# Reordering the operations of a head pair in a threshold attention kernel: turning back and normalization first, v product among the transposes

## The chip, the cores and the metric

The kernel runs on one core of one Trainium2 chip. The metric is the device time of one execution in microseconds, median of three runs; lower is better. TensorE (PE in the rows) multiplies matrices and transposes, VectorE (DVE), ScalarE (ACT) and GpSimd (POOL) work element by element, SyncE (SP) issues most DMA transfers. Each engine works through its own queue in program order.

## The reference

Two stages follow each other. The first is an attention whose weights below a threshold are set to zero, the second sends each token through one of eight small networks, chosen by a hash of its id.

```python
# q, k, v: (8, 8, 576, 64) f32; tau = 0.02
scores = matmul(q, k.T) / sqrt(64)
scores = where(scores >= max(scores) - tau, scores, -1e9)
attn = exp(scores - max(scores))
attn = attn / (sum(attn) + 1e-9)
x = (attn @ v) as (batch * seq, heads * head_dim)   # 4608 x 512
for e in range(8):                                   # expert = hash(token id) % 8
    out[mask_e] = relu(x[mask_e] @ w1[e]) @ w2[e]    # 512 -> 1024 -> 512
```

## The kernel before

The attention half takes two heads of one batch at a time: a head pair p, 32 of them. The 576 rows of q are cut into five steps s: step 0 holds the last 64 rows of both heads, stacked to 128 partitions (one "head" of work), steps 1 to 4 hold 128 rows of each head (two heads of work). The steps of all pairs form one sequence n = 5p + s, and the loop over n is a software pipeline that is written out by hand: each engine gets its instructions in the order in which the loop body names them. One pass of the loop body does work of several ages:

- `score(n + 1)` on TensorE: 288 columns at a time into the PSUM tile sc, of which there are two (line 168).
- `negate(n)` on VectorE: reads sc, writes the negated scores ns and their minimum nmx (line 180); GpSimd makes the threshold thr from it (line 184).
- `expo(n, j)` on ScalarE: w = exp of ns (line 191).
- `mask(n - 1, j)` on VectorE: sets weights beyond thr to zero and sums the rest into rs (line 204).
- `turn_w(n - 2, j)` on TensorE: ten transposes of 64 columns into the one PSUM tile tr (line 215); `put_wT` on ScalarE copies tr to wT_a (steps 0 to 2) or wT_b (steps 3 and 4) (line 233).
- `av_part(p - 1, g, chunks)` on TensorE: the product with v for the pair before, in two groups g (0 with wT_a, 1 with wT_b) over five chunks of keys, into the PSUM tile av, one bank for each group (line 241). `put_oT` on ScalarE copies a finished group to oT (line 247).
- `turn_o` on TensorE, in step 0: transposes oT of the pair p - 2 back into the same tile av (line 215). `put_x(p - 2)`, at the end of step 0, adds 1e-9 to the sums (line 256), takes the reciprocal rec (line 258), multiplies on VectorE to xm (line 261) and on ScalarE, twice, to xt (line 268), and stores xm and xt on SP to x_scratch in DRAM (lines 270, 273).

There is one tile av, and it is used in turn for the product of a pair and for what is turned back. SP also loads q, k and v of later pairs, in step 0, and GpSimd scales q of the next pair in step 1 (line 148). From n = 7 on, each pass ends with one piece of the routing computation (`route`), mostly on VectorE; four of its pieces also put two multiplications of 128 x 648 elements on GpSimd (line 396), and four put nine matmuls into tr. The pieces end in pair 6. After the loop, the experts' half gathers rows of x_scratch and is a long series of matmuls (lines 537 and 551).

Of the kernel before, what the change touches and what calls it, by code (L numbers as in the profile page):

```python
# [9 lines left out]
FP32 = mybir.dt.float32  # L10
# [4 lines left out]
ALU = mybir.AluOpType  # L15
# [5 lines left out]
def kernel(  # L21
# [12 lines left out]
    nc = tc.nc  # L34

    B, H, D, S = qT.shape
    N, DIN = out.shape
    E, _, F = w1.shape
    P = 128
    HP = H // 2  # L40
    NP = B * HP
# [7 lines left out]
    TAIL = NQ * P  # L49
# [15 lines left out]
    x_dram = nc.dram_tensor("x_scratch", (N, DIN), FP32, kind="Internal").ap()  # L65
# [32 lines left out]
    with tc.tile_pool(name="a_q", bufs=1) as a_q, \  # L98
# [21 lines left out]

        oT = a_o.tile([P, 64 + S], FP32, name="oT")
        av = ps_av.tile([P, 2, 512], FP32, name="av")
        kts, rss, scs, nss, stats, ws = {}, {}, {}, {}, {}, {}

        def load_pair(p):
            b, hp = divmod(p, HP)
# [24 lines left out]
        def heads(n):  # L151
            return 1 if n % NS == 0 else 2

        def score(n):


            p, s = divmod(n, NS)
            q_sb, k_sb = q_bufs[p % 3], kts[p]
            for j in range(heads(n)):
                sc = ps_sc.tile([P, 2, 512], FP32, name="sc")  # L160
                scs[n, j] = sc
            for i in range(2):
                for j in range(heads(n)):
                    if s == 0:
                        rows, cols = slice(0, P), slice(TAIL, TAIL + P)
                    else:
                        rows, cols = slice(64 * j, 64 * j + 64), slice(P * (s - 1), P * s)
                    nc.tensor.matmul(scs[n, j][:, i, 0:S2], lhsT=q_sb[rows, cols],  # L168
                                     rhs=k_sb[rows, S2 * i:S2 * i + S2], start=True, stop=True)

        def negate(n):

            nmx = a_st.tile([P, 2], FP32, name="nmx")
            thr = a_st.tile([P, 2], FP32, name="thr")
            stats[n] = (nmx, thr)
            for j in range(heads(n)):
                sc = scs.pop((n, j))
                ns = a_ns.tile([P, S], FP32, name="ns")
                nss[n, j] = ns
                nc.vector.tensor_scalar(out=ns[:].rearrange("p (i s) -> p i s", i=2),  # L180
                                        in0=sc[:, :, 0:S2], scalar1=-1.0, scalar2=None,
                                        op0=ALU.mult, op1=ALU.min, accum_out=nmx[:, j:j + 1])
            nj = heads(n)
            nc.gpsimd.tensor_scalar(out=thr[:, 0:nj], in0=nmx[:, 0:nj], scalar1=drop[:],  # L184
                                    scalar2=None, op0=ALU.add)

        def expo(n, j):
            w = w_bufs[w_count[0] % NW]
            w_count[0] += 1
            ws[n, j] = w  # L190
            nc.scalar.activation(w[:, 0:S], nss[n, j][:], AF.Exp, bias=stats[n][0][:, j:j + 1],  # L191
                                 scale=-1.0)
# [27 lines left out]
        def turn_w(n, j):  # L220
            tr = ps_tr.tile([P, 2, 512], FP32, name="tr")
            turn(tr, ws.pop((n, j)), KCOLS)
            return tr

        def put_wT(n, j, tr):
            s = n % NS
            src = tr[:, :, 0:64 * NC].rearrange("p r (c q) -> p r c q", c=NC)
            if s == 0:
                dst = wT[0][:, :, :, 0:64]
            else:  # L230
                c0 = 64 + P * (s - 1) if s < 3 else P * (s - 3)
                dst = wT[s // 3][:, j, :, c0:c0 + P].rearrange("p c (r q) -> p r c q", r=2)
            nc.scalar.copy(dst, src)  # L233

        def av_part(p, g, chunks):


            width = (WA, WB)[g]
            for c in chunks:
                for j in range(2):  # L240
                    nc.tensor.matmul(av[64 * j:64 * j + 64, g, 0:width],  # L241
                                     lhsT=v_bufs[p % 3][:, c, 64 * j:64 * j + 64],
                                     rhs=wT[g][:, j, c, :], start=(c == 0), stop=(c == NC - 1))

        def put_oT(g):
            c0, width = ((64, WA), (64 + WA, WB))[g]
            nc.scalar.copy(oT[:, c0:c0 + width], av[:, g, 0:width])  # L247
# [1 line left out]
        def turn_o():  # L249
            turn(av, oT, [(P * (t + 1), P * (t + 1)) for t in range(NQ)] + [(64, 0)])  # L250

        def put_x(p):

            b, hp = divmod(p, HP)
            rec = a_st.tile([P, 9], FP32, name="rec")
            nc.vector.tensor_scalar(out=rec[:], in0=rss.pop(p)[:], scalar1=1e-9, scalar2=None,
                                    op0=ALU.add)
            nc.vector.reciprocal(rec[:], rec[:])
            xm = a_x.tile([P, NQ, P], FP32, name="xm")
            xt = a_x.tile([P, D], FP32, name="xt")  # L260
            nc.vector.tensor_tensor(
                out=xm[:].rearrange("p t (j d) -> p t j d", j=2),
                in0=av[:, :, 0:4 * D].rearrange("p j (t d) -> p t j d", t=NQ),
                in1=rec[:, 0:8].rearrange("p (t j) -> p t j", j=2)[:, :, :, None]
                .to_broadcast([P, NQ, 2, D]), op=ALU.mult)
            for j in range(2):
                half = slice(64 * j, 64 * j + 64)
                nc.scalar.mul(xt[half, :], av[half, j, 4 * D:5 * D], rec[half, 8:9])  # L268
            r0, c0 = b * S, hp * P
            nc.sync.dma_start(  # L270
                out=x_dram[r0:r0 + TAIL, c0:c0 + P].rearrange("(t p) m -> p t m", p=P), in_=xm[:])
            for j in range(2):
                nc.sync.dma_start(out=x_dram[r0 + TAIL:r0 + S, c0 + D * j:c0 + D * j + D],
                                  in_=xt[64 * j:64 * j + 64, :])

        def route():

# [106 lines left out]
            for c0 in range(0, NTC, M):  # L384
# [25 lines left out]
                else:  # L410
# [10 lines left out]
                          in_=bass.AP(tensor=tau.tensor, offset=0, ap=[[0, P], [1, 1]]))  # L421
        for q_sb in q_bufs:
# [6 lines left out]
                          in_=bass.AP(tensor=dataclasses.replace(token_ids.tensor,  # L429
                                                                 shape=[2 * N], dtype=I32),  # L430
                                      offset=0, ap=[[2 * NTC, P], [2, NTC], [1, 2]]))
# [4 lines left out]
                                op0=ALU.is_ge)  # L436
        nc.vector.tensor_scalar(out=drop[:], in0=keep_any[:], scalar1=-3e38, scalar2=3e38,
                                op0=ALU.mult, op1=ALU.add)
# [17 lines left out]
        LAST = NS * NP  # L456
        pieces = route()
        with tc.manual_schedule():
            for xg in xg_bufs:
                nc.gpsimd.memset(xg[:], 0.0)  # L460
            score(0)
            for n in range(LAST + NS + 1):
                p, s = divmod(n, NS)
                m = n - 2
                if s == 0 and p + 2 < NP:
                    load_pair(p + 2)
                if s == 0 and p + 1 < NP:
                    load_v(p + 1)
                if s == 1 and p + 1 < NP:
                    scale_q(p + 1)  # L470
                if s == 2 and p in (20, 24):
                    load_w1(p // 4 - 5)
                if s == 2 and p in (22, 26):
                    load_w2((p - 22) // 4)

                done = p - 1
                av_ok = 0 <= done < NP
                if av_ok and s in (1, 2):
                    av_part(done, 0, ((0, 1), (2, 3, 4))[s - 1])
                if av_ok and s in (3, 4):  # L480
                    av_part(done, 1, ((0, 1, 2), (3, 4))[s - 3])
                back = p - 2 if s == 0 else -1
                if back >= 0:
                    turn_o()

                turned = 0 <= m < LAST
                if turned:
                    tr = turn_w(m, 0)
                if n < LAST:
                    negate(n)  # L490
                    expo(n, 0)
                if turned:
                    put_wT(m, 0, tr)
                if n < LAST and heads(n) == 2:
                    expo(n, 1)
                if n + 1 < LAST:
                    score(n + 1)
                if 0 < n <= LAST:
                    for j in range(heads(n - 1)):
                        mask(n - 1, j)  # L500
                if av_ok and s in (2, 4):
                    put_oT(s // 2 - 1)
                if turned and heads(m) == 2:
                    tr = turn_w(m, 1)
                    put_wT(m, 1, tr)
                if back >= 0:
                    put_x(back)
                if n >= NS + 2:
                    next(pieces, None)

    with tc.tile_pool(name="m_x", bufs=2) as m_x, \
# [78 lines left out]
        with tc.For_i(0, n_ov, 1) as it:  # L590
# [5 lines left out]
                out=w1_sb[:],  # L596
                in_=w1[bass.ds(ex, 1)].rearrange("o (c p) f -> p (o c) f", p=P))
# [45 lines left out]
```

## Time and profile before

| | |
|---|---|
| time, median of 3 runs | 1199.1 us (1198.03 to 1199.86) |
| profiled execution: time, span | 1200.82 us, 1199.2 us |
| PE busy | 1082.9 us, 90% |
| DVE busy | 527.9 us, 44% |
| ACT busy | 482.4 us, 40% |
| POOL busy | 256.1 us, 21% |
| mean granted TensorE clock | 0.98 |

The profile shows one execution. The shares are over the whole span; the attention half ends around 605 us, the rest is the experts' half, in which TensorE is busy nearly all the time. So the shares of the attention half have to be read from its own stretch, and the order of waits from single pairs. A busy time of TensorE includes the modelled end of the last matmul of a series, so the distance between the starts of two groups says more than the busy time of one.

### The profile page before, as it was taken

How to read it: one execution, taken by the hardware profiler on the slowest of the kernel's cores; microseconds unless marked ns; L12 is line 12 of the kernel's file. 1: busy time of each engine (PE TensorE's matmuls, PEld its weight loads, DVE VectorE, ACT ScalarE, POOL GpSimd, SP SyncE). 2: the span in 40 equal slices, each digit the busy share in tenths (PEclk: the TensorE clock that was granted, in tenths of full speed). 3: DMA queues.
4: the chain of work that ended last, by engine and by line, in shares of the span. 5: the costliest groups of instructions: out<-in, count | busy, mean ns of one | idle time of the engine just before them, and what ended most of it. 6: DMA issues, size and time to landing. Idle time of an engine off the chain costs nothing. (4 is left out here: it accounts for less than half of the span.)

```text
span 1199.2 us, 19456 instructions
## 1 busy us (share of the span) xinstructions
PE 1082.9 (90%) x7494; PEld 652.3 (54%) x7494; DVE 527.9 (44%) x1390; ACT 482.4 (40%) x777; POOL 256.1 (21%) x305
## 2 busy tenths in 40 slices
PE   6888888888888888888769999999999999999995
PEld 4555555555555555555446465565746556474652
DVE  6899877877787887887511001010110101001000
ACT  4667677777777777777600000001000010000000
POOL 4235322322222222322150201112020110100000
PEclk9899999999999999999879999999999999999998
DMA  3121222221223243420041323322132331110000
GB/s 111 40 79 43 74 64 63 80 71 52 80 70 122 84 136 123 149 75 27 21 126 37 113 76 114 108 97 86 36 130 87 114 107 70 43 65 27 13 18 23
DMA packets 75133, 91.50 MB, mean 76 GB/s; under 512 B 15132, under 2 KB 49948, under 8 KB 75040
## 3 DMA queue, kind: packets, MB, share of 16 engines
q1 hardware_dynamic: 68640, 71.36, 18.9%
q0 software_dynamic: 6400, 18.88, 4.7%
q8 instruction: 60, 0.98, 0.3%
q14 instruction: 33, 0.27, 0.1%
HBM read 72.39 MB, written 19.92 MB: 77 GB/s over the span
## 5 line engine op out<-in xcount | busy, mean ns | idle before, releaser
L551 PE MATMUL o_ps<-w_sb,h_sb 128*128 128x512 f32 x640 | 280.6, 592 | 0.0
L537 PE MATMUL h_ps<-xT,w_sb 128*128 128x320 f32 x1024 | 278.2, 434 | 0.0
L180 DVE TENSOR_SCALAR_CACHE_REDUCE ns<-sc 128x576 f32<-128x576 f32 x288 | 207.7, 754 | 98.8 <-PE sc L168 97.3
L537 PEld LDWEIGHTS h_ps<-xT,w_sb 128*128 128x128 f32 x1024 | 195.3, 191 | 83.7 <-issue 4.1
L191 ACT ACTIVATE w<-ns,nmx 128x576 f32<-128x576 f32 x288 | 224.0, 778 | 34.9 <-DVE ns L180 32.0
L204 DVE SCALAR_TENSOR_TENSOR w<-ns,thr,w 128x576 f32<-128x576 f32 x288 | 228.1, 826 | 0.0
L168 PE MATMUL sc<-k_sb,q 64*128 64x288 f32 (+1 forms) x1152 | 204.5, 430 | 8.7 <-POOL q L148 7.7
L184 POOL TENSOR_SCALAR thr<-nmx,drop 128x2 f32<-128x2 f32 (+1 forms) x160 | 117.9, 737 | 400.0 <-DVE ns L180 400.0
L551 PEld LDWEIGHTS o_ps<-w_sb,h_sb 128*128 128x128 f32 x640 | 118.9, 190 | 136.0 <-issue 135.8
L215 PEld LDWEIGHTS tr<-ident,w 64*128 64x128 f32 x2880 | 115.9, 140 | 108.6 <-ACT wT_a L233 43.0
L215 PE MATMUL tr<-ident,w 64*128 64x64 f32 x2880 | 153.5, 233 | 9.3 <-ACT wT_a L233 6.5
L545 DVE TENSOR_SCALAR h_sb<-h_ps 128x640 f32<-128x640 f32 x32 | 26.4, 825 | 299.6 <-PE h_ps L537 299.6
L554 ACT COPY o_sb<-o_ps 128x512 f32<-128x512 f32 x40 | 23.4, 586 | 300.5 <-PE o_ps L551 300.5
L241 PE MATMUL av<-wT_a,v 128*64 128x320 f32 x640 | 105.2, 460 | 41.7 <-ACT xt L268 41.7
L233 ACT COPY wT_a<-tr 128x640 f32<-128x640 f32 x160 | 110.7, 692 | 65.9 <-PE tr L215 63.3
L168 PEld LDWEIGHTS sc<-k_sb,q 64*128 64x128 f32 (+1 forms) x1152 | 117.3, 194 | 32.7 <-POOL q L148 7.7
L543 ACT ACTIVATE h_sb<-h_ps 128x640 f32<-128x640 f32 x32 | 22.5, 704 | 234.6 <-PE h_ps L537 215.4
L530 DVE COPY xT<-xT_ps 128x512 f32<-128x512 f32 x40 | 27.6, 690 | 194.6 <-PE xT_ps L529 194.6
L233 ACT COPY wT_b<-tr 128x640 f32<-128x640 f32 x128 | 88.5, 691 | 60.3 <-PE tr L215 60.1
L241 PE MATMUL av<-wT_b,v 128*64 128x256 f32 x640 | 83.2, 390 | 24.9 <-ACT oT L247 24.7
L521 POOL DMA_INDIRECT xg<-x_scratch,gidx x40 | 41.2, 1029 | 292.0 <-PE xT_ps L529 265.5
L555 POOL DMA_INDIRECT out_dram<-o_sb,gidx x40 | 40.0, 1000 | 228.1 <-ACT o_sb L554 216.1
(86 smaller groups left out, 374.2 us busy)
## 6 DMA issues: line engine op xcount, KB each, us to landing
w_sb<-in_moe_w_dram SPq DMA_DIRECT2D x16, 2048.0 KB, 9.3
k_sb<-in_k_dram SPq DMA_DIRECT2D x32, 288.0 KB, 2.9
q<-in_q_dram SPq DMA_DIRECT2D x32, 256.0 KB, 3.2
v<-in_v_dram SPq DMA_DIRECT2D x32, 256.0 KB, 3.8
x_scratch<-xm SPq DMA_DIRECT2D x32, 256.0 KB, 2.3
q<-in_q_dram SPq DMA_DIRECT2D x64, 16.0 KB, 2.1
v<-in_v_dram SPq DMA_DIRECT2D x32, 32.0 KB, 3.4
x_scratch<-xt SPq DMA_DIRECT2D x64, 16.0 KB, 1.8
```

Source lines behind the costliest of these rows:

```text
L168: nc.tensor.matmul(scs[n, j][:, i, 0:S2], lhsT=q_sb[rows, cols], rhs=k_sb[rows, S2 * i:S2 * i + S2], start=True, stop=True)
L180: nc.vector.tensor_scalar(out=ns[:].rearrange("p (i s) -> p i s", i=2), in0=sc[:, :, 0:S2], scalar1=-1.0, scalar2=None, op0=ALU.mult, op1= ...
L184: nc.gpsimd.tensor_scalar(out=thr[:, 0:nj], in0=nmx[:, 0:nj], scalar1=drop[:], scalar2=None, op0=ALU.add)
L191: nc.scalar.activation(w[:, 0:S], nss[n, j][:], AF.Exp, bias=stats[n][0][:, j:j + 1], scale=-1.0)
L204: nc.vector.scalar_tensor_tensor(out=w[:, 0:S], in0=nss.pop((n, j))[:], scalar=stats[n][1][:, j:j + 1], in1=w[:, 0:S], op0=ALU.is_le, op1= ...
L215: nc.tensor.transpose(dst[:, r, 64 * c:64 * c + 64], src[rows, c0:c0 + P], ident[rows, rows])
L233: nc.scalar.copy(dst, src)
L241: nc.tensor.matmul(av[64 * j:64 * j + 64, g, 0:width], lhsT=v_bufs[p % 3][:, c, 64 * j:64 * j + 64], rhs=wT[g][:, j, c, :], start=(c == 0) ...
L521: nc.gpsimd.indirect_dma_start(out=xg[:], out_offset=None, in_=x_dram[:, :], in_offset=bass.IndirectOffsetOnAxis(ap=idx, axis=0), bounds_c ...
L537: nc.tensor.matmul(h_ps[:, i, 0:width], lhsT=w1_sb[:, co, fo * P:fo * P + P], rhs=xT[:, co, i * width:i * width + width], start=(co == 0), ...
L551: nc.tensor.matmul(o_ps[:], lhsT=h_sb[:, fo, kt * P:kt * P + P], rhs=w2_sb[:, fo, :], start=(fo == 0), stop=(fo == FO - 1))
L555: nc.gpsimd.indirect_dma_start(out=out[:, :], out_offset=bass.IndirectOffsetOnAxis(ap=idx, axis=0), in_=o_sb[:], in_offset=None, bounds_ch ...
```

## The change

The five steps get an order of their own:

- In step 0, turning back and the product xt for ScalarE, with its two stores, come first; xm on VectorE, with its store, comes behind the negate of that step. Before, both came at the end of the step, xm first.
- The addition of 1e-9 and the reciprocal move to step 2 of the pair before, so rec is there ahead of time. The addition goes from VectorE to GpSimd.
- Group 0 of the v product is split into three and two chunks instead of two and three. Group 1 moves from ahead of the first turn of steps 3 and 4 to between the two turns.
- The copy to oT moves ahead: in step 2 to behind the first exp, in step 4 to ahead of the second exp.
- In steps 0, 3 and 4 the copy of the first turn goes ahead of the first exp on ScalarE.
- In steps 3 and 4 the scores of the next step come behind the second turn.

```diff
-        def put_x(p):
+        def recip(p):
             rec = a_st.tile([P, 9], FP32, name="rec")
-            nc.vector.tensor_scalar(out=rec[:], in0=rss.pop(p)[:], scalar1=1e-9, scalar2=None,
+            nc.gpsimd.tensor_scalar(out=rec[:], in0=rss.pop(p)[:], scalar1=1e-9, scalar2=None,
                                     op0=ALU.add)
             nc.vector.reciprocal(rec[:], rec[:])
+            recs[p] = rec
+
+        def put_xt(p):
+            rec = recs[p]
+            xt = a_x.tile([P, D], FP32, name="xt")
+            for j in range(2):
+                half = slice(64 * j, 64 * j + 64)
+                nc.scalar.mul(xt[half, :], av[half, j, 4 * D:5 * D], rec[half, 8:9])
...
+        def put_xm(p):
+            rec = recs.pop(p)
             xm = a_x.tile([P, NQ, P], FP32, name="xm")
...
-                if av_ok and s in (1, 2):
-                    av_part(done, 0, ((0, 1), (2, 3, 4))[s - 1])
-                if av_ok and s in (3, 4):
-                    av_part(done, 1, ((0, 1, 2), (3, 4))[s - 3])
-                back = p - 2 if s == 0 else -1
-                if back >= 0:
+                q = p - 1
+                if s == 2 and 0 <= q < NP:
+                    recip(q)
+                if s == 0 and p >= 2:
                     turn_o()
+                    put_xt(p - 2)
+                if s in (1, 2) and 0 <= q < NP:
+                    av_part(q, 0, ((0, 1, 2), (3, 4))[s - 1])
+                if n < LAST and s in (1, 2):
+                    negate(n)
+                    expo(n, 0)
+                if s == 2 and 0 <= q < NP:
+                    put_oT(0)
                 turned = 0 <= m < LAST
                 if turned:
                     tr = turn_w(m, 0)
-                if n < LAST:
+                    put_wT(m, 0, tr)
+                if s in (3, 4) and 0 <= q < NP:
+                    av_part(q, 1, ((0, 1, 2), (3, 4))[s - 3])
+                if n < LAST and s not in (1, 2):
                     negate(n)
                     expo(n, 0)
-                if turned:
-                    put_wT(m, 0, tr)
+                if s == 0 and p >= 2:
+                    put_xm(p - 2)
+                if s == 4 and 0 <= q < NP:
+                    put_oT(1)
                 if n < LAST and heads(n) == 2:
                     expo(n, 1)
-                if n + 1 < LAST:
+                if s in (0, 1, 2) and n + 1 < LAST:
+                    score(n + 1)
+                if turned and heads(m) == 2:
+                    tr = turn_w(m, 1)
+                    put_wT(m, 1, tr)
+                if s in (3, 4) and n + 1 < LAST:
                     score(n + 1)
                 if 0 < n <= LAST:
                     for j in range(heads(n - 1)):
                         mask(n - 1, j)
-                if av_ok and s in (2, 4):
-                    put_oT(s // 2 - 1)
-                if turned and heads(m) == 2:
-                    tr = turn_w(m, 1)
-                    put_wT(m, 1, tr)
-                if back >= 0:
-                    put_x(back)
```

## Rows read from the trace of the kernel before

**Rows 1.** Windows: busy time per engine, clock, DMA; routing pairs, then even pairs.
```profile
core 0: us, PE busy (x) PEld busy (x) DVE busy (x) ACT busy (x) POOL busy (x), PEclk, DMA share, GB/s
48.00:148.50 100.50, 86.59 (x916) 54.61 (x916) 87.68 (x234) 68.10 (x112) 37.99 (x38) 0.95 0.21 60
148.50:574.00 425.50, 365.41 (x4224) 227.97 (x4224) 338.67 (x937) 326.27 (x530) 115.42 (x143) 1.00 0.28 85
```
**Rows 2.** Waits: who waited for whom, us in total, times, longest.
```profile
PE av L241 <- ACT xt L268: 41.7, 30, 1.5
...
PE av L241 <- ACT oT L247: 24.7, 31, 0.8
...
PE av L215 <- ACT oT L247: 6.1, 31, 0.5
```
**Rows 3.** Timeline of TensorE over one even pair: start, us, operation, idle before.
```profile
205.42 1.83 PE L241 MATMUL av<-wT_a,v 128*64 128x320 f32 x12
...
207.55 1.19 PE L168 MATMUL sc<-k_sb,q 64*128 64x288 f32 x8
209.54 1.52 PE L241 MATMUL av<-wT_b,v 128*64 128x256 f32 x12 [0.81 <-ACT oT L247]
...
211.35 1.19 PE L168 MATMUL sc<-k_sb,q 64*128 64x288 f32 x8
212.38 0.51 PE L215 MATMUL tr<-ident,w 64*128 64x64 f32 x10
212.81 1.08 PE L241 MATMUL av<-wT_b,v 128*64 128x256 f32 x8
...
214.28 1.24 PE L168 MATMUL sc<-k_sb,q 128*128 128x288 f32 x4
215.45 0.52 PE L215 MATMUL tr<-ident,w 64*128 64x64 f32 x10
216.13 0.53 PE L215 MATMUL av<-ident,oT 64*128 64x64 f32 x10 [0.16 <-ACT oT L247]
216.82 0.52 PE L215 MATMUL tr<-ident,w 64*128 64x64 f32 x10 [0.16 <-ACT wT_a L233]
...
218.20 0.51 PE L215 MATMUL tr<-ident,w 64*128 64x64 f32 x10
220.09 1.30 PE L241 MATMUL av<-wT_a,v 128*64 128x320 f32 x8 [1.38 <-ACT xt L268]
...
221.68 0.70 PE L168 MATMUL sc<-k_sb,q 64*128 64x288 f32 x4
```
**Rows 4.** Timeline of VectorE: negates and masks of a step, then normalization.
```profile
205.18 0.76 DVE L180 TENSOR_SCALAR_CACHE_REDUCE ns<-sc 128x576 f32<-128x576 f32 x1 [1.79 <-PE sc L168]
...
206.54 0.81 DVE L204 SCALAR_TENSOR_TENSOR w<-ns,thr,w 128x576 f32<-128x576 f32 x1
...
207.28 0.81 DVE L204 SCALAR_TENSOR_TENSOR w<-ns,thr,w 128x576 f32<-128x576 f32 x1
...
217.92 0.22 DVE L258 RECIPROCAL rec<-rec 128x9 f32<-128x9 f32 x1
218.34 0.69 DVE L261 TENSOR_TENSOR xm<-av,rec 128x512 f32<-128x512 f32 x1 [0.20 <-DVE rec L258]
```
**Rows 5.** Timeline of ScalarE: step 2 of an even pair, and the last xt.
```profile
207.81 0.69 ACT L233 COPY wT_a<-tr 128x640 f32<-128x640 f32 x1 [0.86 <-PE tr L215]
208.40 0.78 ACT L191 ACTIVATE w<-ns,nmx 128x576 f32<-128x576 f32 x1
209.08 0.41 ACT L247 COPY oT<-av 128x320 f32<-128x320 f32 x1
...
605.53 0.64 ACT L268 ACTIVATE xt<-av,rec 64x64 f32<-64x64 f32 x2 [1.40 <-DVE xm L261]
```
**Rows 6.** GpSimd: two timeline rows, then all of L184 (min/median/max in ns).
```profile
206.79 0.72 POOL L184 TENSOR_SCALAR thr<-nmx,drop 128x2 f32<-128x2 f32 x1 [3.25 <-DVE ns L180]
...
112.32 3.04 POOL L396 TENSOR_TENSOR hi<-hi,parts_h 128x648 f16<-128x648 f16 x2
...
L184 POOL TENSOR_SCALAR thr<-nmx,drop x160: 288/721/1990, 13.2 to 586.5; 128x2 f32<-128x2 f32 x128, 128x1 f32<-128x1 f32 x32
```

More of the change, by code (lines that the diff above doesn't have):

```diff
@@ L122 @@
         av = ps_av.tile([P, 2, 512], FP32, name="av")
-        kts, rss, scs, nss, stats, ws = {}, {}, {}, {}, {}, {}
+        kts, rss, recs, scs, nss, stats, ws = {}, {}, {}, {}, {}, {}, {}
         def load_pair(p):
@@ L250, in turn_o @@
             turn(av, oT, [(P * (t + 1), P * (t + 1)) for t in range(NQ)] + [(64, 0)])
-        def put_x(p):
-            b, hp = divmod(p, HP)
+        def recip(p):
             rec = a_st.tile([P, 9], FP32, name="rec")
-            nc.vector.tensor_scalar(out=rec[:], in0=rss.pop(p)[:], scalar1=1e-9, scalar2=None,
+            nc.gpsimd.tensor_scalar(out=rec[:], in0=rss.pop(p)[:], scalar1=1e-9, scalar2=None,
                                     op0=ALU.add)
             nc.vector.reciprocal(rec[:], rec[:])
+            recs[p] = rec
+        def put_xt(p):
+            b, hp = divmod(p, HP)
+            rec = recs[p]
[3 more added lines that the diff above has]
+                nc.scalar.mul(xt[half, :], av[half, j, 4 * D:5 * D], rec[half, 8:9])
+            r0, c0 = b * S, hp * P
+            for j in range(2):
+                nc.sync.dma_start(out=x_dram[r0 + TAIL:r0 + S, c0 + D * j:c0 + D * j + D],
+                                  in_=xt[64 * j:64 * j + 64, :])
+        def put_xm(p):
+            b, hp = divmod(p, HP)
+            rec = recs.pop(p)
             xm = a_x.tile([P, NQ, P], FP32, name="xm")
-            xt = a_x.tile([P, D], FP32, name="xt")
             nc.vector.tensor_tensor(
@@ L265, in put_x @@
                 .to_broadcast([P, NQ, 2, D]), op=ALU.mult)
-            for j in range(2):
-                half = slice(64 * j, 64 * j + 64)
-                nc.scalar.mul(xt[half, :], av[half, j, 4 * D:5 * D], rec[half, 8:9])
             r0, c0 = b * S, hp * P
@@ L271, in put_x @@
                 out=x_dram[r0:r0 + TAIL, c0:c0 + P].rearrange("(t p) m -> p t m", p=P), in_=xm[:])
-            for j in range(2):
-                nc.sync.dma_start(out=x_dram[r0 + TAIL:r0 + S, c0 + D * j:c0 + D * j + D],
-                                  in_=xt[64 * j:64 * j + 64, :])
         def route():
@@ L474 @@
                     load_w2((p - 22) // 4)
-                done = p - 1
-                av_ok = 0 <= done < NP
-                if av_ok and s in (1, 2):
-                    av_part(done, 0, ((0, 1), (2, 3, 4))[s - 1])
-                if av_ok and s in (3, 4):
-                    av_part(done, 1, ((0, 1, 2), (3, 4))[s - 3])
-                back = p - 2 if s == 0 else -1
-                if back >= 0:
-                    turn_o()
+                q = p - 1
+                if s == 2 and 0 <= q < NP:
+                    recip(q)
+                if s == 0 and p >= 2:
+                    turn_o()
+                    put_xt(p - 2)
[6 more added lines that the diff above has]
+                    put_oT(0)
                 turned = 0 <= m < LAST
```

## The prediction

> **What bounds the kernel now.** I read four views. First the windows [rows 1]: in the long even stretch of the attention half, 425.5 us hold 4224 matmuls. A head pair has 176 (36 for scores, 90 turning weights, 40 for the v product, 10 turning back), so this is 24 pairs of 17.73 us each. TensorE is busy for 365.4 of the 425.5 us, VectorE for 338.7, ScalarE for 326.3: 77 to 86%, none is full. So the pair is not bound by one engine's work but by hand-offs, and the question is whose waits set the 17.73 us.
>
> Second, the list of waits [rows 2]: TensorE's v product waits for xt 41.7 us in all, 30 times, and for the copy to oT 24.7 us, 31 times; turning back waits 6.1 us for oT. Third, one pair on TensorE [rows 3]: the reader should see that from 205.42 to 221.68 its groups follow each other at fixed distances, apart from these places: the v product at 209.54 idles 0.81 behind oT, turning back at 216.13 idles 0.16, the turn behind it 0.16, and the v product at 220.09 idles 1.38 behind xt. By starts the losses are larger than by idle time: sc to v product is 2.0 us (207.55 to 209.54) where sc to a turn is 1.03 (211.35 to 212.38); turn to v product is 1.89 (218.20 to 220.09) where it is 0.43 elsewhere (212.38 to 212.81). Fourth, the neighbours' spacing [rows 4 to 6], which says how early they could deliver.
>
> Both long waits come from program order on ScalarE. xt is its last operation in step 0, behind the copy of the second turn, and the one tile av can't be overwritten before. oT at 209.08 stands behind the second exp of step 2 and ends at 209.49; the product starts at 209.54, so a hand-off takes 0.05. This product writes the other half of av, yet it waits.
>
> **The change, part by part.** *TensorE.* Nothing is added or removed, 176 matmuls stay. I sum the new order from the distances in [rows 3], leaving the waits out.
> Step 0: turning back to first turn 0.43 (ten transposes, as ahead of a v product); first turn to second turn with scores between 1.38 (216.82 to 218.20); turn to product 0.43. Sum 2.24.
> Step 1: product of three chunks, turn, to scores 2.13 (205.42 to 207.55, the same 12 matmuls); scores to turn 1.03; turn to product 0.43. Sum 3.59.
> Step 2: two chunks, turn, to scores 1.59 (220.09 to 221.68); scores to the next step's turn 1.03. Sum 2.62.
> Step 3: turn to product 0.43; three chunks, turn, to scores 1.81 (209.54 to 211.35); scores to turn 1.03. Sum 3.27.
> Step 4: turn to product 0.43; two chunks, turn, to scores 1.47 (212.81 to 214.28); scores to turning back 1.17 (214.28 to 215.45). Sum 3.07.
> Floor of a pair on TensorE alone: 14.79 us, 2.94 under today.
>
> *Who comes late next.* I walk the other engines along that floor, with time 0 at turning back in step 0. Spacings: negate 0.68 (two in 205.18 to 206.54), mask 0.74 (206.54 to 207.28), xm 0.69, of which I count 0.62, as of the mask's 0.81 [rows 4]; copy of a turn 0.59, exp 0.68 and a turn's 0.52 plus a hand-off until its copy starts, about 0.6 [rows 3, 5].
> Negate of step 0 runs at 0.1, right behind the scores. xt needs turning back, 0.53, so 0.58 to 1.22 (0.64, [rows 5]). Does xm wait for xt? They share no data, both only read av. Yet in the last pair xt sat idle 1.40 us until xm was done [rows 5]; so the order of reads counts, and after the change it is xm that waits: 1.27 instead of 0.8. (The Trainium skill, page "PSUM — Partial Sum Buffer", section "PSUM bank collisions raise a hardware error", says that any two engines on one bank and quadrant must be kept apart, two readers as well; the row agrees. Without the rule the pair would come to about 15.0 instead of the 15.3 below.)
> VectorE goes on: xm to 1.9, two masks to 3.4, the two negates of step 1 at 3.4 and 4.0, the single mask to 5.46. TensorE overwrites av at 2.4, so xm (done at 1.96) no longer holds it up; the 1.38 is gone. The scores issued at 4.5 need the second negate's buffer at 4.8, where their second head is due at 4.7: about 0.15 late.
>
> *The reciprocal.* The addition of 1e-9 moves to GpSimd, and VectorE's reciprocal (0.22, [rows 4]) waits for it at the head of step 2, with the two negates queued behind it, and behind them the exp, oT, the turn's copy and TensorE. GpSimd gets to the addition only after thr of step 1, and thr takes 0.72 beside a mask, ending at 207.51, 0.23 after the mask's spacing ends [rows 4, 6]: 5.7 here. The shortest thr is 0.288, the median 0.721, the longest 1.99 [rows 6]; the addition is as small, and VectorE then stands still, so I take the short end, 0.3, with 0.72 as the upper bound. Reciprocal at 6.05, negates at 6.3 and 6.95, while the scores were ready at 5.9. The old place had the addition on VectorE for some 0.2 and no wait on another queue.
> Then exp 7.1 to 7.75, oT (0.41, of which I count 0.36, as 0.68 of exp's 0.78; it now stands ahead of the copy of the turn), that copy 8.11 to 8.80, and step 3's turn at 8.85, where TensorE could do it at 8.72. In step 3 and 4 ScalarE's chain (copy, exp, exp, copy; copy, exp, oT, exp, copy) delivers its last copies 0.05 and 0.16 late. The wait for oT ahead of the product in step 3 is gone: oT ends at 8.2 and the product starts at 9.3.
> Walk: 14.79 + 0.15 + 0.13 + 0.05 + 0.16 = 15.28, so 15.3. With the addition at 0.72 the chain ends 0.43 later: 15.7.
>
> *Queues.* SP gets the two xt stores ahead of the xm store, three stores as before. Nothing in the attention reads them; what hides them is the rest of that half. In the last pair, where nothing hides them, xt and then xm follow each other as xm and then xt did [rows 5], so the last store starts as late: 0. If SP were late with loads behind them it would show as a scores wait; q, k and v are fetched a pair or more ahead, so 0.
> GpSimd in the routing stretch: in one step the two multiplications L396 (3.04 us, [rows 6]) stand in the queue right ahead of the addition, and VectorE would stand still for up to 3.3 us, once.
>
> **The sum.** 24 even pairs x (17.73 - 15.3) = 58.3. The five pairs with routing pieces take 100.5 us, 20.1 each, with VectorE busy for 87.7 and the granted clock at 0.95 [rows 1]: VectorE has little to give. Bounds: 5 x 1.4 gained if the xt wait goes, 3.3 lost; I take 1 gained. Pair 1 (only the oT wait, 0.8) and the last (xt, 1.4): 2.2. Together 61.5. The profiled execution took 1200.8, 1.7 over the median: 1139.3 in its terms, 1138 in those of the median.
>
> **Rivals.**
> *The floor.* All new waits hide and TensorE runs at 14.8: 24 x 2.94 + 3.2 = 73.8, some 1125. For it: the late arrivals are tenths. Against: VectorE (338.7 / 24 = 14.1 a pair) would be at 95% and ScalarE (13.6) at 92%.
> *VectorE's line takes half back.* Addition at 0.72 or longer, xm behind xt, and one more late hand-off of some 0.6: 15.7 to 16.4 a pair, 24 x 2.03 to 24 x 1.33, and with the 3.2 some 1147 to 1164. For it: VectorE's work of 14.1 a pair leaves it about 1.2 us of slack in 15.3, and two new waits stand in its line.
> *The change doesn't do what it says for xt.* If av stays held by xm as long as it was by xt, only the oT part goes, about 1.0 x 24: some 1175. Against: xm is done 0.4 before TensorE wants av.
> *Slower: the clock.* In the pairs 2 to 6 the granted clock averages 0.95, in the even ones 1.00 [rows 1]. If the new order made waits that let it fall to the lower level, 1.2 of 2.4 GHz, a pair's floor would go to at most 29.6. Above (17.73 - 15.3) / 14.8 = 16% of the even stretch at that level the change loses; at 25% it gives about 1226. For it: the clock did fall somewhere in the routing pairs. Against: the even pairs idle 2.5 us each today and hold 1.00; the new order idles less.
>
> **How the numbers follow.** Forecast 1138, own range 1130 to 1146: 0.58. VectorE's line 0.20, floor 0.12, no xt gain 0.03, clock 0.05, no measurable change 0.02. 0.2% (2.4 us) is about what a measurement tells here from no change. Faster 0.93, same 0.02, slower 0.05. The range takes in the floor and the whole of VectorE's line and leaves out the last three: 1124 to 1164.
>
> **What would show it.** Right: the wait of the v product for xt and that for oT fall from 66 us together to a few; the even pairs take about 15.3 us; a new wait of xm for xt, and of the reciprocal for GpSimd's addition, about half a microsecond a pair each; the page's MoE half unchanged. Wrong: an addition of 0.7 us or more, VectorE without idle time, or PEclk below 9 in the even stretch.

## The result, and the profile after

| | before | after |
|---|---|---|
| median | 1198.63 us of 4 runs (1198.03 to 1199.86) | 1132.84 us of 4 runs (1131.87 to 1138.72) |
| profiled execution: time, span | 1200.82, 1199.2 us | 1131.87, 1130.3 us |
| mean granted TensorE clock | 0.98 | 0.988 |

The ratio is 0.946 [0.9426, 0.9494]: faster by 66 us. The forecast was 1138, its own range 1130 to 1146.

Where the time came from is read by cutting both traces at the same events, the start of turning back in step 0 of a pair:

| stretch | before, us | after, us | difference |
|---|---|---|---|
| start to pair 2 | 42.63 | 40.73 | -1.9 |
| pairs 2 to 6, with routing pieces | 102.65 | 100.59 | -2.1 |
| pairs 7 to 30, 24 even ones | 425.45 | 367.96 | -57.5 |
| pair 31 | 17.72 | 14.48 | -3.2 |
| from there to the last turning back | 15.73 | 11.40 | -4.3 |
| the rest: the end of the last pair and the experts' half | 595.02 | 595.14 | +0.1 |

The even pairs went from 17.73 to 15.33 us each and carry 57.5 of the 68.9 us between the two spans. The windows of the kernel after, columns as in [rows 1], show the even stretch first, then the stretch behind pair 31 (up to the last turning back):

```profile
141.32:509.28 367.96, 367.86 (x4226) 246.47 (x4226) 334.66 (x914) 318.20 (x529) 100.19 (x168) 1.00 0.33 99
523.76:535.16 11.40, 7.93 (x90) 4.54 (x90) 3.19 (x10) 5.28 (x10) 0.48 (x2) 1.00 0.09 27
```

TensorE is now busy for 367.86 of 367.96 us; the same matmuls stood in 425.5 us before [rows 1]. That does not make it an engine at its peak: a matmul that starts late is inside the busy time of the series it belongs to, so the distances of the starts still have to be read. VectorE (334.66) is at 91% of the stretch.

The list of waits after (who waited for whom, us in total, times, longest), against [rows 2]. Of the v product's waits for xt (41.7 us) and for oT (24.7 us) one of 0.5 us for oT is left. Of the following, the first two are new; the last two stood at 4.4 and 0.8 us before:

```profile
DVE rec L257 <- POOL rec L255: 20.3, 30, 3.2
...
DVE xm L277 <- ACT xt L267: 18.5, 28, 8.0
...
PEld sc L168 <- DVE ns L180: 14.6, 20, 2.4
...
PE sc L168 <- DVE ns L180: 7.4, 9, 2.3
```

TensorE's timeline over one even pair after, columns as in [rows 3]:

```profile
248.54 0.52 PE L215 MATMUL av<-ident,oT 64*128 64x64 f32 x10
249.01 0.53 PE L215 MATMUL tr<-ident,w 64*128 64x64 f32 x10
249.38 1.33 PE L168 MATMUL sc<-k_sb,q 64*128 64x288 f32 x8
250.52 0.52 PE L215 MATMUL tr<-ident,w 64*128 64x64 f32 x10
250.97 1.84 PE L241 MATMUL av<-wT_a,v 128*64 128x320 f32 x12
252.74 0.53 PE L215 MATMUL tr<-ident,w 64*128 64x64 f32 x10
253.11 1.30 PE L168 MATMUL sc<-k_sb,q 64*128 64x288 f32 x7
254.13 0.33 PE L215 MATMUL tr<-ident,w 64*128 64x64 f32 x2
254.25 0.40 PE L168 MATMUL sc<-k_sb,q 64*128 64x288 f32 x1
254.30 0.66 PE L215 MATMUL tr<-ident,w 64*128 64x64 f32 x8
254.88 1.30 PE L241 MATMUL av<-wT_a,v 128*64 128x320 f32 x8
256.11 0.53 PE L215 MATMUL tr<-ident,w 64*128 64x64 f32 x10
256.47 1.19 PE L168 MATMUL sc<-k_sb,q 64*128 64x288 f32 x8
257.50 0.51 PE L215 MATMUL tr<-ident,w 64*128 64x64 f32 x10
257.94 1.51 PE L241 MATMUL av<-wT_b,v 128*64 128x256 f32 x12
259.38 0.53 PE L215 MATMUL tr<-ident,w 64*128 64x64 f32 x10
259.75 1.19 PE L168 MATMUL sc<-k_sb,q 64*128 64x288 f32 x8
260.77 0.53 PE L215 MATMUL tr<-ident,w 64*128 64x64 f32 x10
261.23 1.08 PE L241 MATMUL av<-wT_b,v 128*64 128x256 f32 x8
262.25 0.52 PE L215 MATMUL tr<-ident,w 64*128 64x64 f32 x10
262.70 1.24 PE L168 MATMUL sc<-k_sb,q 128*128 128x288 f32 x4
```

No row shows idle time, so the loss is read by starts, against the distances that the prediction summed to a floor of 14.79. From the product of step 2 on (254.88) every distance is the floor's to within 0.03. What is lost lies before: turning back to first turn 0.47 (floor 0.43), first to second turn of step 0 1.51 (1.38), and above all in step 1, where the scores begin at 253.11 and the product behind the second turn at 254.88: 1.77, against 1.03 + 0.43 = 1.46. The row at 254.25 points to the cause: the last matmul of the scores, of the second head, runs after two of the turn's matmuls. The buffer of that head is read by the second negate of step 1, and VectorE's timeline of the same pair has this negate from 252.60 for 0.75 us, past the start of the scores:

```profile
249.78 0.69 DVE L277 TENSOR_TENSOR xm<-av,rec 128x512 f32<-128x512 f32 x1 [0.37 <-ACT xt L267]
250.39 0.86 DVE L204 SCALAR_TENSOR_TENSOR w<-ns,thr,w 128x576 f32<-128x576 f32 x1
...
251.19 0.81 DVE L204 SCALAR_TENSOR_TENSOR w<-ns,thr,w 128x576 f32<-128x576 f32 x1
...
252.60 0.75 DVE L180 TENSOR_SCALAR_CACHE_REDUCE ns<-sc 128x576 f32<-128x576 f32 x1
...
254.62 0.22 DVE L257 RECIPROCAL rec<-rec 128x9 f32<-128x9 f32 x1 [0.53 <-POOL rec L255]
```

xm starts 1.24 after turning back (248.54), waiting for xt; two masks and two negates stand behind it. This chain makes 0.31 of the pair's 0.54 over the floor. Another 0.13 comes in step 0: the second turn (250.52) needs the copy of the first, which stands behind xt on ScalarE:

```profile
249.11 0.64 ACT L267 ACTIVATE xt<-av,rec 64x64 f32<-64x64 f32 x2
...
249.78 0.69 ACT L233 COPY wT_b<-tr 128x640 f32<-128x640 f32 x1
```

### The profile page after: what moved, and what is told of

Read it like the earlier page. It is cut to its first block, busy times and chain, and to the rows that moved or that the text cites. A ratio compares the mean times of both kernels' runs of the same rounds, so it can differ in the third digit from the quotient of the medians.

```text
span 1130.3 us, 19626 instructions
## 1 busy us (share of the span) xinstructions
PE 1083.1 (96%) x7494; PEld 672.1 (59%) x7494; DVE 523.0 (46%) x1358; ACT 473.4 (42%) x777; POOL 236.6 (21%) x337
## 5 line engine op out<-in xcount | busy, mean ns | idle before, releaser
L191 ACT ACTIVATE w<-ns,nmx 128x576 f32<-128x576 f32 x288 | 220.3, 776 | 50.8 <-DVE ns L180 49.7
L168 PE MATMUL sc<-k_sb,q 64*128 64x288 f32 (+1 forms) x1152 | 219.8, 429 | 14.8 <-POOL q L148 7.4
L215 PEld LDWEIGHTS tr<-ident,w 64*128 64x128 f32 x2880 | 123.7, 139 | 93.2 <-ACT wT_a L233 33.4
L184 POOL TENSOR_SCALAR thr<-nmx,drop 128x2 f32<-128x2 f32 (+1 forms) x160 | 104.0, 650 | 354.3 <-DVE ns L180 352.5
L215 PE MATMUL tr<-ident,w 64*128 64x64 f32 x2880 | 163.4, 233 | 6.6 <-ACT wT_a L233 2.9
L168 PEld LDWEIGHTS sc<-k_sb,q 64*128 64x128 f32 (+1 forms) x1152 | 132.7, 191 | 39.3 <-DVE ns L180 14.6
L241 PE MATMUL av<-wT_a,v 128*64 128x320 f32 x640 | 101.3, 446 | 0.0
```

The lines of the kernel that those rows point to most:

```text
L215: nc.tensor.transpose(dst[:, r, 64 * c:64 * c + 64], src[rows, c0:c0 + P], ident[rows, rows])
L241: nc.tensor.matmul(av[64 * j:64 * j + 64, g, 0:width], lhsT=v_bufs[p % 3][:, c, 64 * j:64 * j + 64], rhs=wT[g][:, j, c, :], start=(c == 0) ...
```

## The experiments

The theory: two hand-offs in ScalarE's queue cost before (xt last in step 0, oT last in steps 2 and 4), and their removal is the gain. Rivals: the gain needs the new places of the v product and of the copies too; and within the 15.33, the loss comes from GpSimd's addition or from xm's place on VectorE. Twelve kernels were run, each against the kernel before on its own chip (medians there 1198.9 to 1199.94). "Even pair" is the mean of the 24.

**1 to 3. The two hand-offs, one by one and together, from the kernel before.** `e1_norm_only` takes the three new functions of the change and calls them in the old order of everything else:

```diff
+                if s == 2 and 0 <= done < NP:
+                    recip(done)
                 if back >= 0:
                     turn_o()
+                    put_xt(back)
...
                     negate(n)
                     expo(n, 0)
+                if back >= 0:
+                    put_xm(back)
...
-                if back >= 0:
-                    put_x(back)
```

`e2_ot_only` moves only the copies to oT, `e3_norm_and_ot` is both:

```diff
                     expo(n, 0)
+                if av_ok and s == 2:
+                    put_oT(0)
                 if turned:
                     put_wT(m, 0, tr)
+                if av_ok and s == 4:
+                    put_oT(1)
                 if n < LAST and heads(n) == 2:
                     expo(n, 1)
...
-                if av_ok and s in (2, 4):
-                    put_oT(s // 2 - 1)
```

> The kernel before with the first part of the change alone: xt right behind turning back, xm behind the negate, the reciprocal in step 2 with the addition on GpSimd. Theory of the prediction (order on ScalarE decides, and a moved operation pushes what stands behind it): the wait of the v product for xt goes from 41.7 us to under 5, but xt now delays the copy of the first turn, so the second turn of step 0 comes about 0.6 later; gain about 0.9 us in each of 24 even pairs, some 1175 us. Rival (the listed wait is worth its full size): 1.4 us in 30 pairs, 1155 us.

> The kernel before with the earlier copies to oT alone (behind the first exp of step 2, ahead of the second exp of step 4). Theory: the product of group 1 follows the scores after about 1.0 us instead of 2.0, and the two waits of 0.16 around turning back go; gain about 1.1 to 1.3 us in 30 pairs, some 1164 to 1168 us. Rival: the listed 24.7 us are all that is there, or less, since the wait hides a later one: 1175 us or more.

> Both parts together in the kernel before; the pieces of the v product, the copies of the first turn and the scores stay where they were. Theory: the two gains add up, some 1142 to 1148 us, and what is left to the changed kernel (1133) belongs to copying the first turn ahead of the first exp in step 0. Rival (placing the v product between the transposes is what pays): 1160 us or more.

| | us | ratio | even pair |
|---|---|---|---|
| e1_norm_only | 1180.73 | 0.984 [0.9824, 0.9857] | 17.01 |
| e2_ot_only | 1174.25 | 0.9786 [0.977, 0.9803] | 16.87 |
| e3_norm_and_ot | 1153.34 | 0.9622 [0.9597, 0.9647] | 16.11 |

Each removes its wait. The first gives 0.72 a pair, where the wait was 1.4; the second 0.86, about the idle time of its wait (24.7 / 31 = 0.80) and less than the 1.1 to 1.3 that was expected by starts. All three kernels are 5 to 6 us slower than the theory had them, and e2 lies at its rival's 1175. In the first, xt and an exp now stand ahead of the copy in step 0, and its second turn comes 2.10 after the first (before 1.38 [rows 3]). In the second, oT ahead of the second exp of step 4 pushes that step's last copy, and the first turn of step 0 waits 0.53 for it. The gains add (0.72 + 0.86 = 1.58, together 1.62). So the two hand-offs are worth 46 of the 66 us, and 0.78 us a pair belongs to the rest of the change. TensorE's timeline of e3 shows where it is: at turns that wait for ScalarE's copy of the turn before.

```profile
237.64 0.47 PE L215 MATMUL av<-ident,oT 64*128 64x64 f32 x10
238.64 0.53 PE L215 MATMUL tr<-ident,w 64*128 64x64 f32 x10 [0.53 <-ACT wT_a L233]
...
240.70 0.53 PE L215 MATMUL tr<-ident,w 64*128 64x64 f32 x10 [0.51 <-ACT wT_b L233]
```

**4. The change with the v product at its old places.** In `e4_v_pieces_back` group 1 stands ahead of the first turn again, and group 0 is split two and three; the rest is the change.

```diff
                 if s in (1, 2) and 0 <= q < NP:
-                    av_part(q, 0, ((0, 1, 2), (3, 4))[s - 1])
+                    av_part(q, 0, ((0, 1), (2, 3, 4))[s - 1])
+                if s in (3, 4) and 0 <= q < NP:
+                    av_part(q, 1, ((0, 1, 2), (3, 4))[s - 3])
...
                     put_wT(m, 0, tr)
-                if s in (3, 4) and 0 <= q < NP:
-                    av_part(q, 1, ((0, 1, 2), (3, 4))[s - 3])
```

> The changed kernel with the pieces of the v product back at their old places and in the old split (two and three chunks; group 1 ahead of the first turn). Theory: TensorE's floor of a pair stays within 0.2 us, nothing waits for the pieces: 1129 to 1138 us. Rival (the pieces hide the copy of the first turn in steps 3 and 4): about 1 us a pair more, 1155 us or more.

Measured: 1206.24 us, 1.0056 [1.0039, 1.0073], even pair 17.89. The expectation was far off: this one part undone takes back the whole gain. TensorE's timeline, step 3:

```profile
266.01 1.52 PE L241 MATMUL av<-wT_b,v 128*64 128x256 f32 x12
267.45 0.52 PE L215 MATMUL tr<-ident,w 64*128 64x64 f32 x10
268.82 0.53 PE L215 MATMUL tr<-ident,w 64*128 64x64 f32 x10 [0.84 <-ACT wT_a L233]
```

Between the two turns TensorE has nothing left, since the change has put the scores behind the second. It stands for 0.84 until the first turn is copied, in step 3 and again in step 4: +1.01 each by starts. The remaining 0.54 comes from the split: with two chunks in step 1 TensorE reaches that step's scores sooner, and waits there for the negate. The product between the turns is the cover that the scores gave up: the scores behind both turns cost without it. The other way round (product between the turns, scores there too) was not run.

**5 to 7. What holds the pair at 15.33.** `e5_add_on_vector` puts the addition of 1e-9 back on VectorE; `e6_mask_first` puts the first mask of step 0 ahead of xm, where VectorE idled; `e7_mask_and_add` is both.

```diff
-            nc.gpsimd.tensor_scalar(out=rec[:], in0=rss.pop(p)[:], scalar1=1e-9, scalar2=None,
+            nc.vector.tensor_scalar(out=rec[:], in0=rss.pop(p)[:], scalar1=1e-9, scalar2=None,
```

```diff
+                ms = [(n - 1, j) for j in range(heads(n - 1))] if 0 < n <= LAST else []
                 if s == 0 and p >= 2:
+                    if ms:
+                        mask(*ms.pop(0))
                     put_xm(p - 2)
...
-                if 0 < n <= LAST:
-                    for j in range(heads(n - 1)):
-                        mask(n - 1, j)
+                for a in ms:
+                    mask(*a)
```

> The changed kernel with the addition of 1e-9 back on VectorE, in front of the reciprocal in step 2. Theory A (as in the prediction's walk: the reciprocal's wait of 0.53 us is on the line that ends last): 0.3 us in each of 24 even pairs and the single stall of 3.2 us in the routing pairs, some 1122 us. Theory B (in the even pairs the copy of the turn of step 2 waits for the turn, not for VectorE, so the wait is hidden there): only the routing pairs gain, 3 to 6 us, 1127 to 1130 us, even pairs at 15.3 us.

> The changed kernel with the first mask of step 0 ahead of xm instead of behind it, so that it fills the 0.37 us in which xm waits for xt. Theory (the negates of step 1 come late by xm's wait, and the scores of step 1 wait for them): even pairs at about 15.0 us, some 1126 us. Rival (xm, now later, holds av and the v product of step 1 waits): 1133 us or more.

> Both edits in the changed kernel: first mask ahead of xm, addition on VectorE. If the gains of the two single edits add up, some 1120 to 1123 us. Floor by TensorE's own distances: even pairs at 14.8 us, which would be 1117 us.

| | us | ratio | even pair |
|---|---|---|---|
| e5_add_on_vector | 1128.19 | 0.9406 [0.9393, 0.9419] | 15.33 |
| e6_mask_first | 1123.58 | 0.9378 [0.936, 0.9397] | 15.02 |
| e7_mask_and_add | 1119.59 | 0.933 [0.9314, 0.9346] | 15.02 |

The wait for GpSimd's addition, 0.53 in every even pair, costs nothing there: without it the pair is the same to the hundredth. It does cost in the routing pairs. There VectorE's timeline of the kernel after has

```profile
106.14 0.82 DVE L401 TENSOR_TENSOR hi<-iota_h,parts_h 128x648 f16<-128x648 f16 x1
...
110.12 0.22 DVE L257 RECIPROCAL rec<-rec 128x9 f32<-128x9 f32 x1 [3.17 <-POOL rec L255]
```

and with the addition on VectorE pair 7 begins at 137.95 instead of 141.32, 3.4 earlier (pairs 2 to 6 take 95.89 instead of 100.59, the stretch ahead of them 1.33 more). Xm's place does cost in the even pairs: with the mask in its gap, 0.31 a pair. VectorE's timeline of e6:

```profile
230.28 0.81 DVE L204 SCALAR_TENSOR_TENSOR w<-ns,thr,w 128x576 f32<-128x576 f32 x1
...
231.02 0.68 DVE L277 TENSOR_TENSOR xm<-av,rec 128x512 f32<-128x512 f32 x1
...
231.62 1.01 DVE L204 SCALAR_TENSOR_TENSOR w<-ns,thr,w 128x576 f32<-128x576 f32 x1
```

The mask runs straight behind the negate, and xt is done when xm comes. In total time the gains add, and e7 is the best complete version: 13 us under the change, 0.2 a pair over the floor.

**8 and 11. xt by itself.** `e8_no_xt` leaves the two multiplications for xt out and stores a constant tile of zeros for the last 64 rows; `e11_no_xt_scale_late` moves the scaling of q on GpSimd from step 1 to step 3 as well.

```diff
+        xt_c = a_o.tile([P, D], FP32, name="xt_c")
+        nc.vector.memset(xt_c[:], 0.0)
...
-            xt = a_x.tile([P, D], FP32, name="xt")
-            for j in range(2):
-                half = slice(64 * j, 64 * j + 64)
-                nc.scalar.mul(xt[half, :], av[half, j, 4 * D:5 * D], rec[half, 8:9])
+            xt = xt_c
```

```diff
-                if s == 1 and p + 1 < NP:
+                if s == 3 and p + 1 < NP:
                     scale_q(p + 1)
```

> The changed kernel without the two multiplications to xt: the last 64 rows of each head are stored as zeros, all else stays. Theory (xm waits for xt because both read av): xm starts right behind the negate, its wait is gone, even pairs at 14.9 to 15.1 us, 1123 to 1127 us. Rival (xm waits for something else that comes at the same time, turning back or the negate): xm starts as late as now, even pairs at 15.3, 1133 us.

> The run without xt (the last 64 rows are stored as zeros), with GpSimd's scaling of the next pair's q moved from step 1 to step 3. Theory: xm already starts early there, but the mask behind it ran 1.32 us beside the scaling and gave the gain back; with the scaling elsewhere the mask takes 0.8 and the even pairs come to about 15.0 us, 1124 to 1127 us. Rival (the mask was long for another reason, or the lost time lies elsewhere): even pairs stay at 15.3, 1133 us.

Measured: e8 1133.57 us, 0.9456 [0.9443, 0.9469], even pair 15.33; e11 1123.26 us, 0.936 [0.9347, 0.9373], 14.97. The first missed its expectation, and the timeline of e8, with VectorE and GpSimd together, says why:

```profile
249.87 0.69 DVE L277 TENSOR_TENSOR xm<-av,rec 128x512 f32<-128x512 f32 x1
...
250.47 1.32 DVE L204 SCALAR_TENSOR_TENSOR w<-ns,thr,w 128x576 f32<-128x576 f32 x1
...
250.38 0.80 POOL L148 TENSOR_SCALAR q<-q,keep_any 128x640 f32<-128x640 f32 x1
```

Xm does start straight behind the negate now, 0.79 after turning back instead of 1.24. But the mask behind it then runs beside GpSimd's scaling of q, which began 0.09 ahead of it, and takes 1.32 instead of the 0.86 of the kernel after. With the scaling moved away, the mask of e11 is back at

```profile
232.96 0.81 DVE L204 SCALAR_TENSOR_TENSOR w<-ns,thr,w 128x576 f32<-128x576 f32 x1
```

and the gain shows. The scaling itself, in its new place, begins 0.22 behind another mask (239.41); there that mask keeps its 0.82, and GpSimd's row is the long one:

```profile
239.63 1.27 POOL L148 TENSOR_SCALAR q<-q,keep_any 128x640 f32<-128x640 f32 x1
```

So the wait of xm for xt is worth about 0.35 a pair, and in e8 the contention took that place. The scaling moved in the change with xt kept was not run; the mask beside it there takes 0.86, so it had 0.05 to give.

**9 and 10. The copy of the first turn.** The change puts it ahead of the first exp in steps 0, 3 and 4. `e9_copy_first` adds this edit to e3, `e10_copy_behind` undoes it in the change:

```diff
                     tr = turn_w(m, 0)
+                    if s in (0, 3, 4):
+                        put_wT(m, 0, tr)
...
-                if turned:
+                if turned and s in (1, 2):
                     put_wT(m, 0, tr)
```

```diff
                     tr = turn_w(m, 0)
-                    put_wT(m, 0, tr)
+                    if s in (1, 2):
+                        put_wT(m, 0, tr)
...
                     expo(n, 0)
+                if turned and s in (0, 3, 4):
+                    put_wT(m, 0, tr)
```

> The run with normalization first and the earlier copies to oT (even pairs at 16.10 us), and on top of it the copy of the first turn ahead of the first exp in steps 0, 3 and 4; pieces of the v product and scores at their old places. Theory: in step 0 the second turn waits for that copy, which stood behind xt and an exp, 2.06 us after the first turn instead of 1.38; in steps 3 and 4 the exp is done before the turn, so nothing changes there. Even pairs at about 15.4 us, some 1137 us; what the places of the pieces and scores add is then 0.1 us a pair. Rival (the places of the pieces and of the scores are worth most of what is left): even pairs stay at 15.9 or more, 1149 us or more.

> The changed kernel with the copy of the first turn behind the first exp again in steps 0, 3 and 4. Theory: each exp there waits for a negate that comes after the turn, so the copy and the second turn come late: 0.7 us in step 0, 0.5 in step 3, 1.0 in step 4, even pairs at about 17.4 us, some 1182 us. Rival (only step 0 counts): even pairs at 16.0, some 1149 us.

Measured: e9 1181.41 us, 0.9855 [0.9838, 0.9872], even pair 17.10, so 0.99 a pair worse than e3 where a gain was expected. e10 1189.11 us, 0.9912 [0.9896, 0.9927], 17.27, near the 17.4 expected. ScalarE's timeline of e9:

```profile
241.63 0.69 ACT L233 COPY wT_a<-tr 128x640 f32<-128x640 f32 x1 [1.56 <-PE tr L215]
242.22 1.44 ACT L191 ACTIVATE w<-ns,nmx 128x576 f32<-128x576 f32 x2
```

and of e10:

```profile
231.61 0.77 ACT L191 ACTIVATE w<-ns,nmx 128x576 f32<-128x576 f32 x1 [1.07 <-DVE ns L180]
232.29 0.67 ACT L233 COPY wT_a<-tr 128x640 f32<-128x640 f32 x1
```

In e9 the product still stands ahead of the first turn, so the turn comes late, and ScalarE stands idle for 1.56 in front of its copy, with the exps queued behind it. By starts the pair gains 0.44 in step 0 against e3, as intended, and loses 0.68 at the scores of step 1, 0.44 at the first turn of step 4, which waits for a copy behind those exps, and 0.31 at turning back. In e10 the turn comes early, but its copy waits for an exp whose negate is not there, and TensorE's second turn waits 0.89 for the copy (by starts 1.97 behind the product of step 4, where the kernel after has 1.02). So the copy first pays where the turn is first on TensorE too; here, alone, it cost.

**12.** `e12_best_scale_late` is e7 with the scaling of q at step 3.

> The run with both edits (first mask ahead of xm, addition on VectorE; 1119.6 us, even pairs at 15.01), with GpSimd's scaling of q in step 3. TensorE sets the pace of that run by its own distances but for some 0.1 us in step 0, so theory: even pairs at 14.9 to 15.0, no more than 2 us gained, 1117 to 1120 us. Rival (VectorE, whose mask beside the scaling took 1.01 us, still sets the pace): even pairs at 14.8, 1114 us. If the scaling in step 3 makes the scores of step 4 wait: slower, 1125 us or more.

Measured: 1120.93 us, 0.9338 [0.9318, 0.9359], even pair 15.02: no different from e7. With the mask ahead of xm, the contention costs nothing more.

## Why the prediction was right, and where it was not

**The floor** held. From the product of step 2 to the end of the pair every distance was that of [rows 3] to within 0.03, though the groups stand in another order.

**The even pairs**: 15.3 foreseen, 15.33 measured; 58.3 us foreseen, 57.5 measured. But the 0.54 over the floor is made of other terms than those of the walk. The step "0.15 late" (scores of step 1 waiting for the second negate) was right in place and measured 0.31. The waits of 0.37 and 0.53 were there as described, and xm began at 1.24 after turning back against 1.27. The step that failed is *The reciprocal*, "Walk: 14.79 + 0.15 + 0.13 + 0.05 + 0.16": its 0.13 and ScalarE's 0.05 and 0.16 did not appear at all, since TensorE, late by 0.51 until then, reached step 3's first turn 8.96 after turning back (257.50 less 248.54), and the walk had it ready at 8.85. e5 shows it for the addition: taken away, no change. In their place stood lates of 0.04 and 0.13 in step 0. The sum has no term for them, though its own spacings give one: xt to 1.22, then the copy (0.69) and a hand-off (0.05) put the second turn at 1.96, where TensorE could do it at 0.43 + 1.38 = 1.81. The walk also counts short: by its distances TensorE can do step 3's first turn at 2.24 + 3.59 + 2.62 + 0.15 = 8.60, not 8.72, so the 0.13 would have been 0.25 and the pair 15.4. The forecast of the pair came out by luck: errors of both signs, each under 0.2, cancelled. That xm's place is what held the pair was shown by e6 (0.31 back) and e11 (0.36 back).

**The wait of xm for xt**, on which some 0.3 a pair hung: e8 shows it gone with xt. The Trainium skill, page "PSUM — Partial Sum Buffer", section "PSUM bank collisions raise a hardware error", says that two readers on one bank and quadrant have to be kept apart by the program; the runs agree (0.37 with xt, none without), and e6 shows the wait filled with other work.

**The routing pairs**: 1 foreseen, 2.1 measured; the single stall on GpSimd's multiplications was foreseen at 3.3 and measured 3.17, and without it pairs 2 to 6 took 4.7 less (e5).

**The mis-sized term** of the sum is "Pair 1 and the last: 2.2". These stretches gave 9.4: 1.9 up to pair 2, and 3.2 and 4.3 in the last two, for which the sum had a single term of 1.4, though pair 31 runs the same five steps as the even pairs. Without these 7 us the sum would have been within a microsecond. Part of them may be scatter: the stretch up to pair 2 took 39.95 to 42.16 us in e5 to e8, e11 and e12, so its 1.9 can't be put down to the change. In the stretch behind pair 31 a wait of 1.38 for xt went, but the larger part is TensorE's clock. The window before, against the last one shown of after:

```profile
588.45:604.18 15.73, 11.49 (x90) 5.80 (x91) 2.13 (x9) 4.62 (x9) 0.00 (x0) 0.67 0.07 20
```

The granted clock averaged 0.67 before and 1.00 after, for the same 90 matmuls. The products show it row by row, on TensorE's timeline before:

```profile
592.32 2.40 PE L241 MATMUL av<-wT_a,v 128*64 128x320 f32 x8 [1.38 <-ACT xt L268]
...
597.01 3.47 PE L241 MATMUL av<-wT_a,v 128*64 128x320 f32 x12
```

and after:

```profile
526.84 1.84 PE L241 MATMUL av<-wT_a,v 128*64 128x320 f32 x12
...
530.43 1.30 PE L241 MATMUL av<-wT_a,v 128*64 128x320 f32 x8
```

2.73 us lie in these two products alone. Both kernels idle for over a quarter of this stretch, and what decides its clock stays open: the granted clock was 1.00 there in e3, e5 and e11 too (11.3 to 11.4 us), but 0.87 in e6, e7, e8 and e12 (12.8 to 13.0 us), which differ from the change by little. So some 1.5 of the 4.3 us can't be counted on.

**The rivals.** The floor: not reached, but e7 and e11 come to 15.02 and 14.97, and its argument against, VectorE near 95%, was no obstacle to that (in e7 VectorE is busy for 341.08 of the 360.47 us of the even pairs). VectorE's line: the addition took the short end, 0.25, and of further hand-offs only the copy behind xt was late, by 0.13. No gain from xt: refuted by e1. The clock: 1.00 in the even stretch.

**What the change is.** Its two visible waits are 46 us of it (e3). The other 20 hang on a set of moves that, as far as was tried, only work together: copy first on ScalarE, product between the turns, scores behind both. One of them undone costs 73 (e4) or 56 us (e10); one of them added alone to e3 costs 28 (e9).

## What to carry to other kernels

Where several engines work through queues in program order, a move is judged by walking every queue with the new order, not by the one wait that it removes: one edit of the good order undone cost as much here as the whole change had given. On TensorE, put something between an operation and the one that needs its result copied; on the copying engine, put that copy first only if its source comes first as well. When the walk is done, look for the gap that is left on the engine with the longest chain and fill it with work that is ready (here one mask, 9 us).

## What the hardware showed that was not expected

- VectorE's mask took 1.32 us beside GpSimd's scaling of q and 0.81 without it (e8, e11), so a move on one engine can lengthen an operation on another. The Trainium skill, page "GPSIMD Engine Reference", section "8. Key points", says that GpSimd shares its SBUF interfaces with VectorE, with contention, among other cases, when VectorE's instruction has two SBUF inputs; the mask, which reads ns and w, agrees. Xm, which reads av in PSUM and rec, kept its 0.69 although it ran beside the scaling in the kernel after.
- Which of the two pays depends on who starts first. Where the scaling started first it kept its 0.80, and the mask ended 0.60 to 0.61 after it, whenever the mask had begun (1.32 long in e8, 1.01 in e6, 0.86 in the kernel after). Where the mask started first it kept its 0.81 or 0.82, and the scaling took 1.27 or 1.28 (kernel before, e11, e12).
- In the stretch behind pair 31 the granted clock was 0.67 before and 1.00 after, at about the same busy share (11.49 of 15.73 and 7.93 of 11.40 us); in e7, with the same order on TensorE as in the kernel after, it was 0.87 (9.50 of 12.97 us).
